# Sixteen-row substitution with a level of TensorE products, for four of six groups of a delta-rule kernel

## The chip, the cores and the metric

The kernel runs on one core of one Trainium2 chip. The metric is device time in microseconds (us) of one launch, median of the runs shown. The engines are called PE (TensorE, matmuls; PEld is its weight load), DVE (VectorE), ACT (ScalarE), POOL (GpSimd) and SP (SyncE, which issues most DMAs).

## What is computed

Two blocks, one after the other, in float32. The first is a delta-rule attention with 4 batches × 8 heads, 768 positions and 48 numbers a head:

```python
k_n = k / (norm(k) + 1e-06)
for t in range(S):
    y[:, :, t] = einsum('bhd,bhde->bhe', q[:, :, t], state)
    v_old = einsum('bhde,bhd->bhe', state, k_n[:, :, t])
    state = state + beta_t * einsum('bhd,bhe->bhde', k_n[:, :, t], v[:, :, t] - v_old)
```

The second takes the result as 3072 rows of 384, routes each row to the best of 8 experts by cosine similarity (argmax of softmax logits), and computes `gate * (relu(x @ w1[e]) @ w2[e])` with 1024 hidden numbers for that expert alone.

## The kernel before

**Chunks, groups, units.** The recurrence is solved by chunks of 64 positions (`C`), 12 of them (`m` = 0 to 11). Inside a chunk the values that enter the state solve a triangular system, whose matrix is made of products of keys. It is treated as two halves of 32 rows (`HC`): the inverses of the two diagonal 32×32 blocks are made explicitly, and the 32×32 corner between them is applied as a correction. Two chunks form a group (`g` = 0 to 5). A group holds 2 chunks × 32 heads × 2 halves = 128 blocks of 32×32, one for each of the 128 lanes of DVE. A unit `n` is one chunk of half of the batches; four units make a group, and unit `n` needs the state that unit `n` − 2 left.

**Preparing a group** (`prepare`). The keys are loaded, squared (ACT), summed (DVE), scaled (POOL; chunk 1 on DVE), transposed (PE) and moved out of PSUM by ACT. `gram_diag` makes the 32×32 blocks on PE, in 64 small matmuls a chunk. `to_lanes` (L553) transposes them on DVE, so that each lane has one block. POOL's `lower` (L558, L560) cuts the triangle and sets the diagonal to −1. Then comes the substitution: for each row j from 1 to 30 a `product` (L568) and a `subtract` (L572) on DVE, of (31 − j)·j elements in each lane. `from_lanes` (L580) transposes back, into WT, and two `spread` steps on ACT copy WT, with its two inner dimensions exchanged, into the left and the right half of W, each with a mask.

**A unit** is a chain of PE steps of 16 matmuls, with an engine between each two: `old` (keys by state), `rest` on DVE (R), `solve` with W, Y out on ACT, `fix` with the corner, U out on ACT, `solve_again` with W, Z out on ACT, `update`, and `new_state` on DVE. Beside the chain stand `gram`, `from_state`, `inside`, the transposes of the output rows, the logits, and the routing of every four units (`places`). All helpers of PE record their matmuls at L280 and those of ACT at L283, so steps are told apart by their tiles: R,W is `solve`, U,W `solve_again`, Y,Sx `fix`, Z,K `update`, S,KQ `old` or `from_state`; KQ with 48*32 is `gram_diag` and KQ with 48x96 `gram`.

**The order.** Each step is a task of `Plan.add(engine, busy, more, key, run, …)` with costs and a due key written by hand (`PERIOD`, the time planned for a unit, is 7.5). `Plan.order` walks through them with these costs and writes one fixed order for each engine, which is then executed first in, first out. A task with `hold` may make its engine stand a little for it. PSUM is four pairs of banks, which tasks take and give back. The substitution's tiles X and WT lie in the space of the first expert's `w2` until that is loaded; X has two buffers. X of a group is free for a later one when `from_lanes` has read it.

**After the last unit** the expert lists are completed, tokens are gathered and the expert stage begins (lines from L1190 on); two tiles of expert 0 are computed early, beside the last units (L1048, L1059).

Of the kernel before, what the change touches and what calls it, by code (L numbers as in the profile page):

```python
# [9 lines left out]
F32 = mybir.dt.float32  # L10
I32 = mybir.dt.int32
# [5 lines left out]

C = 64
HC = 32
T = 128  # L20
GROUP = 4
AHEAD_AT = 16
# [120 lines left out]
def kernel(  # L143
# [75 lines left out]
    def carved(n, shape, whole):  # L219
        size = shape[0] * shape[1] * (shape[2] if len(shape) > 2 else 1)  # L220
        return [whole[:, i * size:(i + 1) * size].rearrange(
            "p (a b c) -> p a b c" if len(shape) > 2 else "p (a b) -> p a b",
            **dict(zip("abc", shape))) for i in range(n)]
# [8 lines left out]
    buffers("rn", 2, [2, 2, NP, 2])  # L232
    buffers("rt", 2, [2, 2, NP, 2])
    quots = ac.tile([128, 2, 2, NP, 2], F32, name="quots")
    rings["X"], rings["WT"] = carved(2, [HC, HC], w2_flat), carved(3, [HC, HC], w2_flat)[2:]
    buffers("tmp", 2, [(HC // 2) * (HC // 2)])
    buffers("W", 2, [HC, C])
    buffers("Sx", 3, [H, C])
# [30 lines left out]
    def const(name, shape, dtype=F32):  # L269
        K[name] = ac.tile(shape, dtype, name=name)  # L270
        return K[name]
# [13 lines left out]


    ident = cpool.tile([128, 128], F32, name="ident")
    half_wide = cpool.tile([128, 256], F32, name="half")
    half = half_wide[:, 0:2 * GROUP * H]
    root = ac.tile([128, 1], F32, name="root")  # L290
    tiny = ac.tile([128, 1], F32, name="tiny")
    bt = rings["XC"][0].rearrange("p g r -> p (g r)")[0:40, 0:NM * 2 * C].rearrange("p (m o t) -> p m o t", m=NM, o=2)
# [57 lines left out]
    def masks():  # L350
        prow, col = K["prow"], K["col"]
        trow = const("trow", [128, C], I32)
        nc.vector.tensor_single_scalar(trow, prow, C - 1, op=ALU.bitwise_and)
        col_f = const("col_f", [128, C])
        nc.vector.tensor_copy(col_f, col)
        trow_f = const("trow_f", [128, C])
        nc.vector.tensor_copy(trow_f, trow)
        nc.vector.tensor_tensor(const("upper", [128, 1, C])[:, 0], col_f, trow_f, op=ALU.is_gt)
        nsec = const("nsecond", [128, 1])
        nc.vector.tensor_single_scalar(nsec, trow_f[:, 0:1], float(HC), op=ALU.is_ge)  # L360
        nc.vector.tensor_scalar_mul(nsec, nsec, -1.0)
        nc.vector.tensor_scalar(const("nfirst", [128, 1]), nsec, -1.0, -1.0, op0=ALU.mult, op1=ALU.add)
        for t in rings["Sx"]:
            nc.gpsimd.memset(t[:, :, 0:HC], 0.0)

    def load_beta():
        for i in range(2):
# [59 lines left out]
        return 4 * g * PERIOD  # L427

    def prepare(g):
        ms = (2 * g, 2 * g + 1)  # L430
        t0 = group_key(g)
        for m in ms:
            planned_k(m, t0 - 14 * PERIOD + (m % 2) * 2 * PERIOD if m > 1 else -200.0 + 0.5 * m)
        if g == 0:
            plan.add("SP", 1.6, 2.5, -199.8, load_beta, writes=["bt"])
            plan.add("DVE", 1.0, 0.2, -40.0, masks, reads=["iotas"], writes=["masks"])
            for ms_ in ((0, 1), tuple(range(2, NM))):
# [2 lines left out]
                         writes=[("beta_s", ms_[0])])  # L440
                plan.add("ACT", 0.4, 0.2, -140.0 if ms_[0] == 0 else -60.0, beta_root(slice(ms_[0], ms_[-1] + 1)),
                         reads=[("beta_s", ms_[0]), "half"], writes=[("sqb", a) for a in ms_])
        plan.add("DVE", 0.8, 0.2, t0 - 9.7 * PERIOD, beta_refine(slice(2 * g, 2 * g + 2)), reads=[("beta_s", min(2 * g, 2))],
                 writes=[("sqb", a) for a in ms] + ["quot"])
        ss, rt = buf("rn", g), buf("rt", g)

# [7 lines left out]
                nc.vector.tensor_reduce(ss[:, m % 2].rearrange("p i j jj -> p i (j jj)"), buf("sq", m), axis=AX.X, op=ALU.add)  # L454
            return step
        for m in ms:
            plan.add(*act(768), t0 - 12.5 * PERIOD + (m % 2) * PERIOD, square(m),
                     reads=[("k", m % 4, 0), ("k", m % 4, 1)], writes=[at("sq", m)])
            plan.add(*dve(768), t0 - 12 * PERIOD + (m % 2) * PERIOD, total(m),
                     reads=[at("sq", m)], writes=[at("rn", g) + (m % 2,)])  # L460

        def flat(t, part):
# [28 lines left out]
        for part in (slice(0, 1), slice(1, 2)) if g == 0 else (slice(0, 2),):  # L491
            xs = range(part.start, part.stop)
            those, roots_of = [at("rn", g) + (x,) for x in xs], [at("rt", g) + (x,) for x in xs]
            if g < 2:
                plan.add(*act(16 * len(xs)), t0 - 10 * PERIOD, roots_act(part), reads=those + ["half"], writes=roots_of)
            else:
                plan.add("POOL", 5.5, 0.2, t0 - 10 * PERIOD, roots(part), reads=those + ["half"], writes=roots_of)
            plan.add("DVE", 1.1 if g < 2 else 0.5, 0.2, t0 - 9.6 * PERIOD - (g == 0) * 30, scales(part), hold=g == 0,
                     reads=those, writes=roots_of + ["quots"])
            plan.add("DVE", 0.12 * len(xs), 0.2, t0 - 9.6 * PERIOD, scaled(part), hold=g == 0,  # L500
                     reads=[("sqb", 2 * g + x) for x in xs], writes=roots_of)

        def keys(m):
# [32 lines left out]
                                mm(p[r:r + HC, jj, to:to + w], KQ[rows, i, j, y, hf * HC:(hf + 1) * HC], KQ[rows, i, j, y, c:c + w])  # L536
            return step_
        for m in ms:
            plan.add(*(dve(850) if m == 1 else pool(768)), t0 - 9.2 * PERIOD + (m % 2) * PERIOD, keys(m), hold=g == 0,
                     reads=[("k", m % 4, 0), ("k", m % 4, 1), at("rt", g) + (m % 2,)], writes=[at("K", m)])  # L540
            plan.add(*pe(8, 0.11), t0 - 8.6 * PERIOD + (m % 2) * PERIOD, transposes("K", m, "KT"), mode=2,
                     reads=[at("K", m), "ident"], take=("KT", m))
            plan.add(*act(1024), t0 - 8.4 * PERIOD + (m % 2) * PERIOD, out_of_psum(m, "KT", slice(0, C)),
                     reads=[("psum", ("KT", m))], writes=[at("KQ", m) + ("K",)])
        for m in ms:
            first = m % 2 == 0
            plan.add(*pe(64, 0.02), t0 - 7.2 * PERIOD, gram_diag(m), mode=1, reads=[at("KQ", m) + ("K",)],
                     writes=[("X_next", g % 2)] + ([] if first else [("psum", ("diag", g))]),
                     take=("diag", g) if first else None)
        X = buf("X", g)  # L550

        def to_lanes():
            nc.vector.transpose(X, pair(("diag", g)).rearrange("p jj (x c) -> p c jj x", c=HC))  # L553
        plan.add(*dve(1024), t0 - 6.5 * PERIOD, to_lanes, hold=g == 0, reads=[("psum", ("diag", g))],
                 writes=[at("X", g), ("X_next", g % 2)])

        def lower():
            nc.gpsimd.affine_select(out=X, in_=X, compare_op=ALU.is_ge, fill=0.0, base=-1,  # L558
                                    pattern=[[1, HC], [-1, HC]], channel_multiplier=0)
            nc.gpsimd.memset(X.rearrange("p a b -> p (a b)")[:, ::HC + 1], -1.0)  # L560
        plan.add("POOL", 1.2, 0.1, t0 - 6.4 * PERIOD, lower, writes=[at("X", g)])

        for j in range(1, HC - 1):
            rows = HC - 1 - j
            t = buf("tmp", j)[:, 0:rows * j].rearrange("p (a b) -> p a b", b=j)

            def product(j=j, rows=rows, t=t):
                nc.vector.tensor_tensor(t, X[:, j + 1:, j:j + 1].broadcast_to([128, rows, j]),  # L568
                                        X[:, j:j + 1, 0:j].broadcast_to([128, rows, j]), op=ALU.mult)

            def subtract(j=j, rows=rows, t=t):
                nc.vector.tensor_tensor(X[:, j + 1:, 0:j], X[:, j + 1:, 0:j], t, op=ALU.subtract)  # L572
            key = t0 - (6.0 - j * 4.0 / HC) * PERIOD
            plan.add("DVE", rows * j / 960 + 0.085, 0.13, key, product, reads=[at("X", g)], writes=[at("tmp", j)], hold=g == 0)
            plan.add("DVE", rows * j / 960 + 0.085, 0.13, key + 0.01, subtract, reads=[at("tmp", j)], writes=[at("X", g)], hold=g == 0)

        WT, W = buf("WT", g), buf("W", g)

        def from_lanes():
            nc.vector.transpose(WT, X)  # L580
        plan.add(*dve(1024), t0 - 1.9 * PERIOD, from_lanes, reads=[at("X", g)], writes=[at("WT", g), ("X_next", g % 2)])
        for b, name in enumerate(("nfirst", "nsecond")):
            def spread(b=b, name=name):
                act_copy(W[:, :, b * HC:(b + 1) * HC], WT.rearrange("p i x -> p x i"), K[name])
            plan.add(*act(1024, True), t0 - 1.8 * PERIOD, spread, reads=[at("WT", g), "masks"], writes=[at("W", g) + (b,)])

    def x_of(m, jj, i, j):
        return ((jj * 2 + m % 2) * 2 + i) * NP + j
# [496 lines left out]
    for g in range(NG):  # L1085
# [5 lines left out]
        if g == NG - 1:  # L1091
            for i in range(NF, NF + 2 * KC):
                plan.add("SP", 0.4, 2.5, group_key(NG - 2) + 4.0 * i, first_weights(i),
                         writes=["w1_first"] + [("k", a, b) for a in range(4) for b in range(2)])
            for i in range(NF):
                plan.add("SP", 0.4, 2.5, group_key(NG - 1) + 2.0 * i, first_weights(i),
                         writes=["w2_first", ("X", 0), ("X", 1), ("WT", 0)])
        for n in range(4 * g, 4 * g + 4):
            unit(n)
            if n == groups[group_of[n]["n"]]["first"] + group_of[n]["G"] - 1:  # L1100
# [6 lines left out]
                early_tile(i, unit_key(AHEAD_AT + 6) + 2 * i * PERIOD)  # L1107
    def warm(p):
        for b in range(2):
            mm(p[HALF[b], b, 0:256], ident[:, HALF[b]], half_wide)  # L1110
    plan.emit(warm)
    lists = {-1: lists[groups[-1]["n"]]}
    att.close()
# [279 lines left out]
```

## Time and profile before

| | us |
|---|---|
| runs | 618.40, 620.38, 622.43 |
| median | 620.38 |
| profiled execution, its time | 617.46 |
| profiled execution, its span | 615.6 |
| first `solve` of unit 0 | 66.71 |
| first matmul of the expert stage (L1190) | 344.48 |
| mean granted PE clock, share of full speed | 0.900 |

The profile is one execution. Times in it count from its span's start. A group's row has the engine, the operation, out<-in by the program's names, partitions x elements, the count, the busy time in us and the mean duration in ns, then the idle time of the engine just before and what ended it; "issue" is idle time for which the profile shows no cause. One PE record is one pass: a step of 16 float32 matmuls has 32. "w_first" in a name is the space of the first expert's weights, where k, X and WT lie. The rows around the first use of the substitution, in order of time on DVE:

```profile
27.80 1.25 DVE L553 STREAM_TRANSPOSE w_first<-psum_pair 128x1024 f32<-128x1024 f32 x1 [1.79 <-PE psum_pair L280]
...
32.73 0.13 DVE L568 TENSOR_TENSOR tmp<-w_first 128x30 f32<-128x30 f32 x1
...
58.24 1.24 DVE L553 STREAM_TRANSPOSE w_first<-psum_pair 128x1024 f32<-128x1024 f32 x1
...
60.66 0.19 DVE L572 TENSOR_TENSOR w_first<-w_first,tmp 128x30 f32<-128x30 f32 x1
...
61.37 1.23 DVE L580 STREAM_TRANSPOSE w_first<-w_first 128x1024 f32<-128x1024 f32 x1
```

The first line fills the lanes of group 0, the third those of group 1, and the last takes group 0 back. On ACT the two spreads of group 0 follow at 62.64 (2.07 us) and 64.61 (2.04 us).

### The profile page before, as it was taken

The page shows a single profiled execution, that of the slowest core. Times are in us where ns is not written, and L with a number is a line of the kernel's source. Part 1 is how long each engine was busy: PE and PEld are TensorE (multiplying, and loading weights), DVE is VectorE, ACT ScalarE, POOL GpSimd, SP SyncE. Part 2 cuts the span into 40 slices and gives each one's busy share as a digit, 9 for nine tenths or more (in the row PEclk, how much of TensorE's full clock was granted, in tenths as well). Part 3 has the DMA queues.
Part 4 walks back from the last instruction along what each step waited for, and adds up shares of the span by engine and source line. Part 5 has one row for each costly group of instructions (what it writes and reads, how often), then busy time and mean ns, then how long its engine had stood idle before and what let it go on. Part 6 is the DMA issues. An engine that isn't in the chain of part 4 may idle for free. (4 is left out here: it accounts for less than half of the span.)

```text
span 615.6 us, 21947 instructions
## 1 busy us (share of the span) xinstructions
PE 516.1 (84%) x9643; PEld 425.9 (69%) x9643; DVE 275.9 (45%) x778; ACT 185.4 (30%) x343; POOL 168.5 (27%) x228
## 2 busy tenths in 40 slices
PE   3573688688797878888899599999999999999990
PEld 3462577578686767777887577887767777777870
DVE  4798777777789877962325121111011221121000
ACT  2331534634635536555442020111001221110110
POOL 4433426064534132230212212331202211111100
PEclk9965678667879897998899799999999999999996
DMA  4444734543341340032201599997637666679300
GB/s 81 75 82 82 198 72 71 105 99 70 65 100 32 90 135 18 19 101 66 85 31 43 184 383 384 382 370 256 227 139 245 187 207 237 209 254 338 131 15 18
DMA packets 116334, 90.55 MB, mean 147 GB/s; under 512 B 83394, under 2 KB 105308, under 8 KB 116226
## 3 DMA queue, kind: packets, MB, share of 16 engines
q1 hardware_dynamic: 110722, 77.76, 42.7%
q0 software_dynamic: 4416, 11.06, 5.1%
q8 instruction: 80, 1.31, 0.9%
q10 hardware_dynamic: 1088, 0.20, 0.2%
q14 instruction: 28, 0.23, 0.1%
HBM read 77.06 MB, written 12.13 MB: 145 GB/s over the span
## 5 line engine op out<-in xcount | busy, mean ns | idle before, releaser
L1200 PEld LDWEIGHTS acc<-xTm,w 128*128 128x128 f32 x576 | 77.7, 191 | 5.8 <-issue 1.8
L1202 ACT ACTIVATE hT<-acc 128x512 f32<-128x512 f32 (+3 forms) x52 | 28.5, 548 | 175.2 <-PE acc L1200 175.2
L1200 PE MATMUL acc<-xTm,w 128*128 128x128 f32 (+3 forms) x576 | 80.3, 299 | 0.0
L1217 PE MATMUL acc<-w,hT 128*128 128x384 f32 (+2 forms) x272 | 78.9, 489 | 0.0
L572 DVE TENSOR_TENSOR w_first<-w_first,tmp 128x30 f32<-128x30 f32 (+9 forms) x180 | 69.0, 385 | 3.9
L568 DVE TENSOR_TENSOR tmp<-w_first 128x30 f32<-128x30 f32 (+9 forms) x180 | 66.7, 372 | 4.1
L280 PE MATMUL psum_pair<-KQ 48*32 48x64 f32 (+2 forms) x2304 | 50.0, 265 | 18.9 <-issue 9.2
L1230 POOL DMA_INDIRECT out_dram<-y,more_ids x22 | 21.7, 986 | 160.5 <-DVE y L1220 127.4
L1217 PEld LDWEIGHTS acc<-w,hT 128*128 128x128 f32 (+2 forms) x272 | 42.2, 176 | 30.3 <-issue 5.8
L1191 DVE COPY xTm<-acc 128x384 f32<-128x384 f32 (+3 forms) x26 | 12.6, 508 | 109.1 <-PE acc L1190 104.5
L280 PEld LDWEIGHTS psum_pair<-KQ 48*32 48x32 f32 (+1 forms) x2304 | 42.4, 135 | 24.4 <-issue 12.1
L1220 DVE TENSOR_SCALAR y<-acc,xg 128x384 f32<-128x384 f32 x20 | 12.4, 618 | 97.7 <-PE acc L1217 93.2
L1200 PEld LDWEIGHTS acc<-xTm,w_first 128*128 128x128 f32 x288 | 44.6, 200 | 3.7 <-DVE y L1227 0.6
L1200 PE MATMUL acc<-xTm,w_first 128*128 128x128 f32 (+3 forms) x288 | 46.8, 325 | 0.4 <-DVE xTm L1191 0.4
L1217 PE MATMUL acc<-w_first,hT 128*128 128x384 f32 (+2 forms) x176 | 44.2, 489 | 0.0
L280 PE MATMUL psum_pair<-S,KQ 48*64 48x64 f32 x1408 | 35.6, 244 | 9.9 <-issue 4.7
L280 PEld LDWEIGHTS psum_pair<-S,KQ 48*64 48x64 f32 x1408 | 30.5, 155 | 13.4 <-issue 6.3
L283 ACT ACTIVATE KQ<-psum_pair 128x1024 f32<-128x1024 f32 x24 | 24.4, 1022 | 43.5 <-PE psum_pair L316 33.7
L973 POOL DMA_INDIRECT idmap<-tokid,slots_i x24 | 24.1, 1005 | 42.3 <-DVE slots_i L949 22.8
L1217 PEld LDWEIGHTS acc<-w_first,hT 128*128 128x128 f32 (+2 forms) x176 | 23.1, 163 | 17.8 <-issue 4.5
L622 POOL TENSOR_TENSOR V<-v,sqb 128x384 f32<-128x384 f32 x24 | 20.9, 876 | 48.8 <-DVE R L677 22.0
L469 POOL TENSOR_TENSOR rt<-rn,half 128x32 f32<-128x32 f32 x4 | 22.0, 5488 | 30.2 <-DVE rn L454 30.2
(207 smaller groups left out, 766.2 us busy)
## 6 DMA issues: line engine op xcount, KB each, us to landing
w<-in_moe_w_dram SPq DMA_DIRECT2D x24, 1536.0 KB
w_first<-in_moe_w_dram SPq DMA_DIRECT2D x10, 1536.0 KB
q<-in_q_dram SPq DMA_DIRECT2D x96, 48.0 KB
v<-in_v_dram SPq DMA_DIRECT2D x48, 96.0 KB
w_first<-in_k_dram SPq DMA_DIRECT2D x88, 48.0 KB
x_dram<-XC SPq DMA_DIRECT2D x5, 800.0 KB
idmap<-space SPq DMA_DIRECT2D x1, 2048.0 KB
w_first<-in_moe_w_dram SPq DMA_DIRECT2D x6, 256.0 KB
```

The source lines that it names most:

```text
L280: nc.tensor.matmul(out_, lhsT=lhsT, rhs=rhs, start=start, stop=True, skip_group_check=True)
L283: nc.scalar.activation(out_, in_, ACT.Copy, scale=scale)
L469: nc.gpsimd.tensor_tensor(out=flat(rt, part), in0=flat(ss, part), in1=half[:, 0:w], op=ALU.pow)
L568: nc.vector.tensor_tensor(t, X[:, j + 1:, j:j + 1].broadcast_to([128, rows, j]), X[:, j:j + 1, 0:j].broadcast_to([128, rows, j]), op=ALU.mult)
L572: nc.vector.tensor_tensor(X[:, j + 1:, 0:j], X[:, j + 1:, 0:j], t, op=ALU.subtract)
L622: nc.gpsimd.tensor_tensor(buf("V", m)[:, i * 2 * NP * D:(i + 1) * 2 * NP * D].rearrange("p (jj j d) -> p jj j d", jj=2, d=D), buf("v", m)[ ...
L973: put = nc.gpsimd.indirect_dma_start(out=idmap[:, :], out_offset=bass.IndirectOffsetOnAxis(ap=slot_i[:, i:i + 1], axis=0), in_=K["tokid"][ ...
L1191: nc.vector.tensor_copy(t.xT[:, :, b * T:b * T + n], psX[:, :, 0:n])
L1200: nc.tensor.matmul(psH[:, i, :], lhsT=t.w1[:, j, (f + i) * 128:(f + i + 1) * 128], rhs=t.xT[:, j, 0:t.width], start=(j == 0), stop=(j == K ...
L1202: nc.scalar.activation(t.hT[:, f:f + k, 0:t.width], psH, ACT.Relu)
L1217: nc.tensor.matmul(psO[c:c + w, :], lhsT=t.hT[:, f, b * T + o:b * T + o + w], rhs=t.w2[:, f, :], start=(f < q), stop=(f >= NF - q))
L1230: nc.gpsimd.indirect_dma_start(out=out[:, :], out_offset=bass.IndirectOffsetOnAxis(ap=t.ids[b][0:n, 1:2], axis=0), in_=y[0:n, :], in_offse ...
```

## The change

For groups 0, 1, 3 and 5 (`FINE`) the substitution runs in the two 16×16 diagonal blocks (`LC`) of each 32×32 block at once: j goes from 1 to 14, and each of the 28 operations covers both blocks, 2·(15 − j)·j elements. The 16×16 corner is then made by PE in two passes of 64 matmuls (`level_one`, `level_two`, each in two halves of 32), with 64 rows, 64 columns of weights and 16 moving columns. Their weights are W itself, filled for a while by ACT with the transposed first rows (`rows_spread`, two copies of 512); the result of the first pass comes out through ACT (`level_one_out`) into WN, and that of the second is added to WT by DVE (`merged`). After that the old spreads fill W. Groups 2 and 4 keep the 30 rows of substitution.

```diff
+LC = 16
+FINE = (0, 1, 3, 5)
-    rings["X"], rings["WT"] = carved(2, [HC, HC], w2_flat), carved(3, [HC, HC], w2_flat)[2:]
+    lanes = HC * HC + HC
+    rings["X"] = [w2_flat[:, 0:lanes]]
+    rings["WT"] = carved(1, [HC, HC], w2_flat[:, lanes:])
+    rings["WN"] = carved(1, [LC, HC], w2_flat[:, lanes + HC * HC:])
...
+        for t in rings["W"]:
+            nc.gpsimd.memset(t, 0.0)
...
+        if fine:
+            for j in range(1, LC - 1):
+                rows = LC - 1 - j
+                t = buf("tmp", j)[:, 0:2 * rows * j].rearrange("p (e a b) -> p e a b", e=2, b=j)
+                def product(j=j, rows=rows, t=t):
+                    nc.vector.tensor_tensor(t, blocks[:, :, j + 1:LC, j:j + 1].broadcast_to([128, 2, rows, j]),
+                                            blocks[:, :, j:j + 1, 0:j].broadcast_to([128, 2, rows, j]), op=ALU.mult)
+                def subtract(j=j, rows=rows, t=t):
+                    to = blocks[:, :, j + 1:LC, 0:j]
+                    nc.vector.tensor_tensor(to, to, t, op=ALU.subtract)
...
+        def rows_from_lanes():
+            nc.vector.transpose(WN, X.rearrange("p a b -> p b a")[:, 0:LC])
         def from_lanes():
+            if fine:
+                nc.vector.memset(X[:, LC:, 0:LC], 0.0)
             nc.vector.transpose(WT, X)
...
+                def rows_spread(b=b, name=name):
+                    act_copy(W[:, :, b * HC:b * HC + LC], WN.rearrange("p r x -> p x r"), K[name])
+            def level_one(xs):
+                    for x in xs:
+                        for o in range(2):
+                            mm(p[HALF[o], 0, x * LC:(x + 1) * LC], W[HALF[o], x], WT[HALF[o], LC:, x])
+            def level_one_out():
+                act_copy(WN.rearrange("p r x -> p (r x)"), pair(level)[:, 0], K["lo"])
+            def level_two(xs):
+                            mm(p[HALF[o], 1, x * LC:(x + 1) * LC], W[HALF[o], x], part[HALF[o], x * LC:(x + 1) * LC])
+            def merged():
+                nc.vector.scalar_tensor_tensor(out=to, in0=pair(level)[:, 1].rearrange("p (x c) -> p x c", c=LC),
+                                               scalar=K["lo"], in1=to, op0=ALU.mult, op1=ALU.add)
+            for a in range(2):
+                plan.add(*pe(32, 0.0335), L1 + 0.03 + a * 0.01, level_one(half_x[a]), reads=both + [at("WT", g)],
+                         writes=[("psum", level)] if a else (), take=None if a else level)
```

To make room for WN, X has one buffer in place of two. The due keys of a fine group's preparation move later by two PERIODs, since its substitution is shorter (`t0 = group_key(g) - (0 if fine else 2) * PERIOD`, with the numbers in the keys lowered by two, so those of groups 2 and 4 stay). A few masks are added, and a constant is made narrower. The planner then writes a new order for every engine: among others SP issues the keys of chunk 3 and 4 after q and v of chunk 0, and POOL clears both W buffers (`memset`) at the beginning.

## Prediction

> **What bounds the kernel now.** I read the page's busy line and slices first, to see where TensorE (PE) is not full.
>
> ```profile
> PE 516.1 (84%) x9643; PEld 425.9 (69%) x9643; DVE 275.9 (45%) x778; ACT 185.4 (30%) x343; POOL 168.5 (27%) x228
> PE   3573688688797878888899599999999999999990
> DVE  4798777777789877962325121111011221121000
> PEclk9965678667879897998899799999999999999996
> ```
>
> A slice is 15.4 us. From about 335 us on PE is at 9: that is the expert stage, which the change doesn't touch and which starts when routing ends. Before that DVE stands at 7 to 9 and PE at 5 to 8, part of it on a low clock. Next come the stages between the first solves of the six groups (a PE step that reads a new W starts each), and the tail.
>
> ```profile
> 0.00:66.70 66.70, 32.13 (x843) 27.19 (x843) 52.02 (x143) 20.33 (x27) 30.62 (x80) 0.76 0.45 80
> 66.70:116.50 49.80, 39.35 (x1292) 34.33 (x1292) 39.20 (x109) 24.25 (x43) 16.79 (x15) 0.81 0.51 113
> 116.50:165.10 48.60, 38.09 (x1280) 34.68 (x1284) 34.75 (x92) 23.74 (x39) 23.39 (x19) 0.75 0.44 91
> 165.10:212.00 46.90, 39.78 (x1422) 35.86 (x1416) 40.29 (x114) 23.30 (x43) 15.10 (x20) 0.90 0.31 73
> 212.00:253.50 41.50, 34.37 (x1307) 30.90 (x1310) 32.25 (x93) 18.78 (x34) 8.90 (x13) 0.84 0.25 62
> 253.50:289.80 36.30, 29.68 (x1140) 27.23 (x1130) 22.03 (x68) 20.37 (x40) 9.91 (x13) 0.95 0.23 72
> 289.80:335.00 45.20, 43.52 (x991) 37.95 (x991) 13.61 (x66) 18.60 (x51) 10.52 (x17) 0.96 0.16 50
> ```
>
> Columns: stretch, length, busy us of PE, weight load, DVE, ACT, POOL, then clock, DMA share, GB/s. Each stage but the last does the four units of one group and prepares a later one. The stage lasts 49.8 us while DVE is loaded and 36.3 when it isn't. Two lines are most of DVE's load:
>
> ```profile
> L572 DVE TENSOR_TENSOR w_first<-w_first,tmp 128x30 f32<-128x30 f32 (+9 forms) x180 | 69.0, 385 | 3.9
> L568 DVE TENSOR_TENSOR tmp<-w_first 128x30 f32<-128x30 f32 (+9 forms) x180 | 66.7, 372 | 4.1
> ```
>
> That is the substitution: 135.7 us, 22.6 a group. The timeline (start, us, engine, line; ACT rows, then PE rows) shows whether it is late.
>
> ```profile
> 112.43 2.09 ACT L283 ACTIVATE W<-w_first,nfirst 128x1024 f32<-128x1024 f32 x1 [2.75 <-DVE w_first L580]
> 114.43 2.02 ACT L283 ACTIVATE W<-w_first,nsecond 128x1024 f32<-128x1024 f32 x1
> ```
>
> ```profile
> 112.72 1.83 PE L316 MATMUL psum_pair<-ident,K 128*128 128x128 f32 x8 [0.71 <-DVE lz L792]
> 116.51 1.13 PE L280 MATMUL psum_pair<-R,W 64*64 64x64 f32 x32 [1.96 <-ACT W L283]
> ```
>
> For group 1 it is: PE stands until W is spread. The W of groups 0 to 5 were spread by 66.7, 116.5, 163.4, 202.1, 244.2 and 279.6, and first used at 66.7, 116.5, 165.1, 212, 253.5 and 289.8: groups 0, 1 and 2 wait on it, 3 to 5 have 9 us or more in hand. So the substitution ends last only in the first half, and later PE's own work does. From 66.7 to 335 PE is idle 43.5 us: 19.1 under "issue", 5.1 for W, 7.4 for Z (ACT, part of it behind the spreads), 6.6 for DVE, the rest small.
>
> **DVE.** For a fine group the 60 operations go. In their place come 28 with 28 to 112 elements; the rows of those sizes give 0.19 (30 elements) to 0.27 us (108) and the timeline 0.03 between them: 7.6 us. Added are a transpose of 512 (half of L580's 1.24: 0.65), a memset of 256 (0.27 at L336) and the merge of 512 out of PSUM (0.68, L659). Net 13.4 us off DVE, 54 over four groups. It counts only where DVE is late.
>
> **The start.** The transpose to lanes still ends at 29.1 and POOL's triangle at 30.7. Then 7.6 us of operations, with two totals (0.95 each), group 1's scales (2.3) and scaling (0.25) queued between them: 42.7. One total belongs to chunk 4, whose k now stands in SP's queue behind q and v of chunk 0 (8 loads take 5.2 us): issued until about 36, squared about 39, so some 2 us of standing, with the rest of the substitution queued behind: 44.7. Transposes and memset to 46.9, ACT's two 512-row spreads (half of 2.08 each) to 47.7. Now PE's order: the four new steps stand among two transposes of K (1.97 each), one of q (1.97) and two gram_diag (2.0 each). 9.9 us of queue, 4.8 of steps (below), 0.9 for the eviction, 0.9 for the merge, 4.1 for the old spreads: 68.5. On a full clock the transposes take 1.04, which saves 2.8: 65.7. I take 66, against 66.65: 0.7 gained of the 14 us that DVE saves; the queue ate it. Bounds 63 and 70. POOL's memset of both W (4096 elements; 512 took 0.52) is 4.2 us inside the 8.9 in which POOL waits before L506, and costs 4 where that gap is gone. The other moved loads have SP's lead as cover.
>
> **Stages 1 to 3.** Group 1's lanes should be filled at about 61 and its triangle be out at 63; 7.6 us of operations follow, with two copies of S between them that wait for units 0 and 1 (74.5 and 77.3 now), so they end near 80; transposes, spreads, four steps between unit steps and the merge make W1 some 15 us later, at 96, 20 us earlier than now. So the stages from 66.7 and 116.5 should fall to that from 212, the one whose W was in time beside a full substitution: 49.8 and 48.6 against 41.5, 15.4 us. That includes the cold run behind the stall (clock 0.50 from about 114 to 132). The stage from 165 has 5.4 over 41.5 with DVE 86% busy; its substitution turns fine; I take half, 2.7. Removed in all: 0.7 + 15.4 + 2.7 = 18.8.
>
> **PE's new work.** 128 matmuls a fine group, two records each (16 matmuls show as x32): 256, each with a load of 64 columns. No row has this shape. Low bound: gram_diag, 16 ns a record; high: the beta transposes, 64 columns with 8 moving, 39 ns.
>
> ```profile
> 176.66 2.14 PE L280 MATMUL psum_pair<-KQ 48*32 48x64 f32 x128
> 183.04 2.02 PE L280 MATMUL psum_pair<-KQ 48*32 48x64 f32 x128
> 10.54 5.55 PE L280 MATMUL psum_pair<-ident,XC 8*64 8x8 f32 x142 [1.15 <-DMA w_first<-in_k_dram]
> ```
>
> That is 4.0 to 10.0 us a group; I take 19 ns, 4.8 us, 1.2 a step, near gram_diag since it too is a run of small tiles on idle quarters. [...] Group 0's steps are in the start. The other three are 14.4 us in stages where PE idles 17% (7.1 of 41.5); the steps wait on one another, so the planner puts unit steps between, and I let half show: 7.2. The bounds are 0 and 30.
>
> **ACT and issue.** 1.04 + 1.04 + 0.65 = 2.7 us more ACT a fine group; unit evictions (Y, U, Z) queue behind, as Z does now (2.9 at 163). Now 7.4 us of Z waits go with 25 us of spreads; 8.1 more us at under that rate: 1.5. "Issue" idle, 19.1 us for some 14,900 PE instructions, grows with 1,536 more: 2.0. One X buffer in place of two serializes groups' substitutions; a fine one between two full ones leaves room (9 us in hand).
>
> **Sum.** 617.46 (span 615.6) − 18.8 + 7.2 + 1.5 + 2.0 = 609.4. The median of the runs, 620.38, is 2.9 above the profiled one: 612.
>
> **The clock.** It can undo this.
>
> ```profile
> 177.00:180.00 3.00, 2.97 (x118) 2.65 (x101) 1.60 (x5) 0.25 (x1) 2.40 (x4) 0.66 0.65 228
> 180.00:183.00 3.00, 3.00 (x97) 2.82 (x97) 2.61 (x6) 1.02 (x1) 1.50 (x3) 0.50 0.24 44
> ```
>
> PE is full here and its clock still falls, after gram_diag's small tiles; 64-wide steps then take 1.1 us, not 0.65. The new steps are small tiles too: one cold run of 8 us, some 4 lost, per group would add 12. [...]
>
> **Rivals.**
> - *DVE bounds all of it*: the stage from 165 gives all 5.4, the start its 3.7, and the new steps vanish in PE's idle time: −24.5 + 3.5, 596.5, as a median 599. For it: stage lengths follow DVE's load. Against: after 165 no W is late and PE idles just 6.6 us for DVE in all stages. 0.20.
> - *Slower, PE throughput*: the steps use two of the four quarters at a time and run at 27 ns, 6.9 a group, all of it shown: 20.7 + 3.5, and only the labelled waits go (5.1 for W, 6.6 for DVE, 3.7 of Z): +9, 627, as a median 629; with the clock's 12 more, 641. It decides from about 20 ns a record fully shown (3 × 5.1 + 3.5 = 18.8). For it: dense PE rows after 165, and the clock. 0.23.
> - *Given back*: W1 is early, but unit 2 and 3 wait behind level steps and spreads, and the 15.4 shrinks to 8: 617, as a median 620. 0.17. That the operations are not replaced is excluded by the order of instructions.
>
> **Numbers.** The forecast has 0.40, its own range 606 to 619. One per cent, 6.2 us, is about what a measurement tells from no change: faster is under 614.2, slower over 626.6. Of the forecast 0.27 falls under and 0.13 within; with the rivals faster 0.47, same 0.30, slower 0.23. 598 to 629 leaves out the slow rival's clock part and the fast one's better half.
>
> **What would show it.** Right: first solve at 63 to 70; W of group 1 spread by 90 to 100; unit 4's solve 8 us or more earlier than 116.5; level steps 1 to 1.5 us each; DVE busy near 222. Wrong: a step over 1.8 us, clock 0.5 behind the steps, or the stages from groups 3 and 5 on longer by more than 5 us.

## The result, and the profile after

The changed kernel took 663.96 us (median of 661.37 to 665.71) against 621.12 (618.40 to 622.43): a ratio of 1.071, 95% interval 1.066 to 1.075. It is slower by 43 us; the prediction said 612. The profiled execution shown here took 664.17, with a span of 662.4.

The busy line and the slices of the changed kernel:

```profile
PE 573.6 (87%) x10667; PEld 486.5 (73%) x10667; DVE 231.4 (35%) x667; ACT 196.0 (30%) x355; POOL 171.4 (26%) x230
PE   3639789888788988788899969999999999999990
DVE  4880563783373693281222241111001212121100
PEclk9999985888695698897868979999999999999996
```

DVE lost 44.5 us of work, for 54 predicted. PE gained 57.5 us and 1,024 records, and the stretch in which PE is not full (slices below 9, before the expert stage) has become longer, not shorter. The expert stage is as long as it was (272.2 us for 271.1); it only starts later, at 390.23 where it started at 344.48: 45.75 us. The stretches between the first solves of the groups say where (columns as in the prediction's table: stretch, length, busy us of PE, weight load, DVE, ACT, POOL, then clock, DMA share, GB/s; the last row ends at the first matmul of the expert stage):

```profile
0.00:78.68 78.68, 47.49 (x1100) 43.54 (x1100) 42.08 (x127) 23.01 (x30) 34.95 (x84) 1.00 0.50 103
78.68:132.80 54.12, 48.66 (x1461) 45.60 (x1464) 32.99 (x81) 24.42 (x40) 11.07 (x8) 0.75 0.30 54
132.80:182.45 49.65, 40.90 (x1380) 37.16 (x1376) 26.36 (x77) 25.17 (x43) 21.91 (x23) 0.79 0.44 89
182.45:239.53 57.08, 50.58 (x1621) 46.95 (x1616) 36.00 (x103) 24.02 (x42) 18.77 (x20) 0.76 0.21 46
239.53:283.73 44.20, 36.04 (x1375) 33.58 (x1369) 18.87 (x57) 21.47 (x39) 10.87 (x15) 0.88 0.29 77
283.73:329.14 45.41, 40.09 (x1295) 37.30 (x1287) 19.00 (x60) 21.75 (x40) 8.99 (x12) 0.85 0.21 63
329.14:390.23 61.09, 54.50 (x1104) 46.29 (x1104) 19.07 (x95) 20.14 (x55) 14.83 (x20) 0.88 0.14 42
```

The rows where a fine group's corner is made are the first, second, fourth and sixth: 78.7, 54.1, 57.1 and 45.4 us for 66.7, 49.8, 46.9 and 36.3. The third, without a corner, is as long as it was (49.7 for 48.6), although DVE has 8.4 us less to do there. The lengths no longer follow DVE's load; they follow PE's.

Two groups of the page show the exchange, the substitution's two-block subtract on DVE, and the corner's matmuls on PE:

```profile
L591 DVE TENSOR_TENSOR w_first<-w_first,tmp 128x28 f32<-128x28 f32 (+6 forms) x56 | 15.3, 273 | 1.4
...
L285 PE MATMUL psum_pair<-w_first,W 64*64 64x16 f32 x1024 | 55.0, 256 | 7.4 <-issue 6.7
```

The first was costed well: with its product (16.6) it is 8.0 us a group, 7.6 predicted. The second is the result. Four groups of 256 records take 55.0 us of PE, 54 ns a record; the prediction had 19. The time up to the expert stage, before and after (columns as above), shows how little hides it:

```profile
0.00:344.48 344.48, 261.79 (x8254) 230.69 (x8254) 238.86 (x708) 149.38 (x275) 118.47 (x177) 0.85 0.35 78
```

```profile
0.00:390.23 390.23, 318.27 (x9278) 290.42 (x9278) 194.37 (x597) 159.98 (x287) 121.40 (x179) 0.85 0.31 69
```

PE is busy 318.3 us where it was busy 261.8 (+56.5), and its idle time only falls from 82.7 to 72.0 (−10.7). These two make the 45.75.

The timeline of PE shows one group's steps (start, us; the first two rows are group 0, the others group 5):

```profile
52.90 3.60 PE L285 MATMUL psum_pair<-w_first,W 64*64 64x16 f32 x64
60.20 3.60 PE L285 MATMUL psum_pair<-w_first,W 64*64 64x16 f32 x64
...
302.48 1.75 PE L285 MATMUL psum_pair<-w_first,W 64*64 64x16 f32 x54 [0.90 <-issue]
304.63 2.04 PE L285 MATMUL psum_pair<-w_first,W 64*64 64x16 f32 x64
308.81 3.43 PE L285 MATMUL psum_pair<-w_first,W 64*64 64x16 f32 x61
```

A half step of 64 records takes 2.0 us at 304.63 and 3.4 us four us later. Windows of 3 us around it show what changed (clock is the number after POOL):

```profile
302.00:305.00 3.00, 2.52 (x69) 2.32 (x70) 0.00 (x0) 0.62 (x2) 0.00 (x0) 1.00 0.21 39
305.00:308.00 3.00, 3.00 (x68) 2.95 (x69) 0.00 (x0) 0.92 (x2) 0.99 (x1) 0.79 0.37 111
308.00:311.00 3.00, 3.00 (x74) 3.00 (x76) 0.17 (x1) 0.49 (x1) 0.97 (x1) 0.50 0.51 136
311.00:314.00 3.00, 3.00 (x76) 3.00 (x76) 0.00 (x0) 0.00 (x0) 0.00 (x0) 0.50 0.03 7
314.00:317.00 3.00, 3.00 (x74) 3.00 (x75) 0.25 (x1) 0.00 (x0) 0.00 (x0) 0.50 0.00 0
```

From 305 on PE is written as busy without a gap, and the granted clock falls from 1.00 to 0.50 and stays there. The records of the half step at 304.63 start 29 ns apart, those of the one at 308.81 53 ns. So a record costs 29 ns on the full clock and 53 on half, and most of the steps run on half: group 3's from 202 to 222, group 1's from 96 to 115, and by its times group 0's too (the clock written for that part is taken up at the end).

### The profile page after: what moved, and what is told of

It reads as the page before. It is cut to its first block, busy times and chain, and to the rows that moved or that the text cites. A ratio compares the mean times of both kernels' runs of the same rounds, so it can differ in the third digit from the quotient of the medians.

```text
span 662.4 us, 23917 instructions
## 1 busy us (share of the span) xinstructions
PE 573.6 (87%) x10667; PEld 486.5 (73%) x10667; DVE 231.4 (35%) x667; ACT 196.0 (30%) x355; POOL 171.4 (26%) x230
## 5 line engine op out<-in xcount | busy, mean ns | idle before, releaser
L285 PE MATMUL psum_pair<-KQ 48*32 48x64 f32 (+2 forms) x2304 | 51.7, 272 | 14.5 <-issue 13.1
L285 PE MATMUL psum_pair<-w_first,W 64*64 64x16 f32 x1024 | 55.0, 256 | 7.4 <-issue 6.7
L285 PEld LDWEIGHTS psum_pair<-w_first,W 64*64 64x64 f32 x1024 | 53.9, 211 | 8.7 <-issue 7.3
L285 PEld LDWEIGHTS psum_pair<-KQ 48*32 48x32 f32 (+1 forms) x2304 | 44.1, 140 | 19.2 <-issue 16.1
L1302 DVE TENSOR_SCALAR y<-acc,xg 128x384 f32<-128x384 f32 x20 | 12.4, 618 | 97.7 <-PE acc L1299 93.2
L285 PE MATMUL psum_pair<-S,KQ 48*64 48x64 f32 x1408 | 38.1, 256 | 7.0 <-issue 4.6
L285 PEld LDWEIGHTS psum_pair<-S,KQ 48*64 48x64 f32 x1408 | 32.9, 165 | 10.6 <-issue 6.0
L520 POOL TENSOR_TENSOR K<-w_first,rt 128x384 f32<-128x384 f32 x22 | 18.2, 848 | 46.0 <-DVE rt L502 24.5
```

The lines of the kernel that those rows point to most:

```text
L285: nc.tensor.matmul(out_, lhsT=lhsT, rhs=rhs, start=start, stop=True, skip_group_check=True)
L520: (nc.vector if m == 1 else nc.gpsimd).tensor_tensor(heads(buf("K", m))[:, i], buf("k", m)[:, i], rt[:, m % 2, i].rearrange("p j jj -> p ( ...
L1302: nc.vector.tensor_scalar_mul(y, psO, t.x[b][:, Dm:Dm + 1])
```

## The experiments

**Theories.** A: the loss is the steps' own PE time, and nothing hides it; a half step takes its records by the time of one tile, over the number of tiles that run at once, and twice that on half clock. B: the loss is the longer way to W, with more tasks in a fixed order over DVE, ACT and PE and one X buffer; PE's time would have fitted into its idle time.

Two of the kernels below compute another corner, and one none. The routing then sees other rows, and the expert stage has another length. For these three only times up to the first matmul of the expert stage are compared ("the start of the experts": 344.48 before, 390.23 after), not the whole.

**The same steps, with few records.** Each half step is two matmuls of 256 moving columns with the weights of one block:

```diff
-                    for x in xs:
-                        for o in range(2):
-                            mm(p[HALF[o], 0, x * LC:(x + 1) * LC], W[HALF[o], x], WT[HALF[o], LC:, x])
+                    h = slice(0, 256) if xs[0] == 0 else slice(256, 512)
+                    q = slice(0, 16) if xs[0] == 0 else slice(16, 32)
+                    for o in range(2):
+                        mm(p[HALF[o], 0, h], W[HALF[o], xs[0]], WT.rearrange("p c x -> p x c")[HALF[o], q, LC:])
```

> The changed kernel with each half step of level_one and level_two made of 2 matmuls of 256 moving columns in place of 32 of 16, the weights being those of one block alone (so the corner of the inverses is not the right one, and routing sees other rows). Every task, its waits, the two spreads of rows and the one X buffer stay; PE work of the steps falls from 1,024 records (55 us in the profile after) to 64. Theory A (the steps' own PE time, with the low clock around them, is the loss): the first matmul of the expert stage comes at 342 to 352 us in place of 390, the total at 615 to 628. Theory B (the loss is the longer way to W: more tasks over DVE, ACT and PE in a fixed order, and one X buffer; the matmuls mostly fill idle PE time): 650 to 664.

The whole took 764.3 us, outside what either theory said, because the other corner sent more tiles to the experts: their matmuls have 960 records on w where the kernel before has 576. I had not thought of that. Up to the experts the run answers the question. Its group and its first expert matmul:

```profile
L285 PE MATMUL psum_pair<-w_first,W 64*64 64x256 f32 x64 | 13.9, 516 | 0.8 <-ACT W L288 0.8
```

```profile
350.89 0.87 PE L1273 MATMUL acc<-ident,xg 128*128 128x128 f32 x3 [4.66 <-DMA xg<-x_dram,ids]
```

With 41.1 us less of PE in the steps, and every task, wait and buffer of the changed kernel still there, the experts start 39.3 us earlier. What is left over the kernel before is 6.4 us. (A second profile of the changed kernel, on another chip, has its steps at 56.9 us and its experts at 387.21: such differences hold to some 3 us.)

**Four quarters instead of two.** The same 1,024 records and columns, but the outputs of odd blocks go to the other half of the partitions, so that all four quarters of the array are used (the corner lands in the wrong place):

```diff
-                            mm(p[HALF[o], 0, x * LC:(x + 1) * LC], W[HALF[o], x], WT[HALF[o], LC:, x])
+                            mm(p[HALF[o ^ (x % 2)], o, x * LC:(x + 1) * LC], W[HALF[o], x], WT[HALF[o], LC:, x])
```

> The changed kernel with the level matmuls writing to the other half of the partitions for every odd block (and to the bank of their row half), so that four quarters of the array follow each other in place of two; count and sizes are the same, the sums go to places that are not read for them (the corner is not the right one). Theory A with the reason that two quarters alone share the work: a record takes 15 ns on the full clock and 28 on the low one, half of now, a half step 1.0 to 1.8 us in place of 1.9 to 3.6, and the total falls by 22 to 30 to 634 to 642. If the weights' load or the issue is the limit whatever the quarter, the steps stay at 1.9 to 3.6 us and the total at 660 to 667. Theory B: 655 to 664 although the steps get shorter.

The steps' group, and one half step on each clock:

```profile
L285 PE MATMUL psum_pair<-w_first,W 64*64 64x16 f32 x1024 | 28.8, 247 | 7.6 <-issue 6.6 <-ACT W L288 0.8
```

```profile
51.91 1.91 PE L285 MATMUL psum_pair<-w_first,W 64*64 64x16 f32 x64
...
282.32 1.12 PE L285 MATMUL psum_pair<-w_first,W 64*64 64x16 f32 x64
```

Half the time for the same records: 1.9 for 3.6 us, 1.1 for 2.0; the records start 26 and 14.5 ns apart, for 53 and 29. From these distances, times the number of quarters, my estimate is that a 64×64 tile with 16 columns holds its quarter for some 105 ns on half clock and 58 on full (4 × 26 and 2 × 53, 4 × 14.5 and 2 × 29). The edit also gives each row half a PSUM bank of its own, where both wrote into one, and no run takes the two apart; but the small tiles below write one bank from four row groups at 16 ns a record, so a shared bank alone does not hold a record for 53. The experts start at 362.14. The three kernels differ in their steps' matmuls alone: 13.9, 28.8, 55.0 us; starts 350.89, 362.14, 390.23. From the first to the second a us of step costs 0.75, from the second to the third 1.07 (0.89 with the second profile). That is A: little of it is hidden. (The whole, 679.3, again has other routing.)

**No fine group** (`FINE = ()`, all the rest of the change kept).

> The changed kernel with no fine group: all six groups with the full substitution, but with one X buffer, the memset of W and the masks of the change. Theory A: what is left of the change costs little, 616 to 630. Theory B in the part of the single X buffer (a group's lanes can be filled only when the group before has gone back, and W comes late): 635 to 660.

628.3 us, ratio 1.016 (1.010 to 1.022): about 10 us of the loss are not the corner's. Its PE has the records of the kernel before (9,643) but is busy 271.4 us up to the experts, not 261.8: it works at a lower clock (0.72 and 0.66 in the second and third stretch, 0.81 and 0.75 before), and is idle 0.8 us longer. Why the clock is lower isn't shown.

**The steps alone, in the kernel before.** 256 such matmuls for each of groups 0, 1, 3 and 5 as soon as their W is whole; only a small copy on DVE reads the result:

```diff
+            for i in range(4):
+                plan.add(*pe(32, 0.0335), t0 - 1.7 * PERIOD + 0.01 * i, level_step(half_x[i % 2], i // 2), reads=both + [at("WT", g)],
+                         writes=[("psum", level)] if i else (), take=None if i else level)
```

> The kernel before with the 256 level matmuls of each of groups 0, 1, 3 and 5 added after W is complete, as PE work that nothing in the computation waits for (one small DVE copy reads their PSUM so that it can be given back); the result is not changed. Theory A: the same 1,024 records cost about as much here, 30 to 50 us: 650 to 670. Theory B: they fill idle PE time and cost under 10: 621 to 631.

687.6 us, 69.5 more than the 618.07 of the kernel before on that chip: more than A said. The experts start 65.7 later: PE is busy 59.4 us longer up to there, of which the steps took 52.2, and idle 6.2 longer. PE's waits for W went from 5.1 to 18.3, since the steps stand in front of units' steps and wait for both spreads; other waits fell by about half of that. A names the greater part; the rest is B's, a wait of the place that I had chosen, and other matmuls that take longer.

The same place with four quarters, and with wide matmuls, separates the two without another routing:

> The kernel before plus 256 matmuls of the level's shape for each of groups 0, 1, 3 and 5, as in the run that took 687.6, but with the outputs in all four quarters of TensorE instead of two. Theory A: a half step falls from 3.5 us to 1.9 at half clock (1.0 at full clock), 22 to 28 us go, 658 to 668 us. Theory B (what costs is where the steps stand in the order and what they wait for): 678 to 690.

> The same, but each half step is two matmuls of 256 moving columns in place of 32 pairs of 16: the same places in the order, the same waits, the same 1,024 columns a step, a twentieth of the records. Theory A: own time 10 to 15 us in all in place of 52, so 630 to 648 us, and the clock after the steps back at 1.00 as it is in the changed kernel with wide matmuls. Theory B: 670 to 690.

This chip ran the kernel before in 635.2 us (630.3 to 639.6); the numbers in the expectations were for the other one, so differences are taken. Quarters: 680.1, +44.9 (ratio 1.065, 1.057 to 1.073), 24.6 less than with two quarters; steps 29.5, W waits 16.2. Wide: 664.3, +29.1 (1.043, 1.036 to 1.050), steps 17.2, W waits 18.3. Steps and added waits for W make 40.6 and 30.4, a rough sum, as other waits change too. The waits for W are nearly the same in all three, and the rest follows the steps' time. The wide steps missed the 10 to 15 us and, in group 1, the clock that the expectation gave them; more on that below.

**Two X buffers**, again with no fine group:

```diff
-    rings["X"] = [w2_flat[:, 0:lanes]]
+    rings["X"] = [w2_flat[:, 0:lanes], w2_flat[:, lanes:2 * lanes]]
...
```

> The changed kernel with no fine group (as in the run that took 628.3) and two X buffers again, WN's place given up. If the 10 us that the run without fine groups lies over the kernel before come from the one X buffer: 615 to 622 us. If they come from the moved loads, the cleared W buffers and the new order: 625 to 631.

637.8 against 635.2: 1.003 (0.999 to 1.007), for 1.016 with one buffer. So most of the 10 us, some 8 (3 to 12 by the two intervals), are the one buffer's; the moved loads, the clearing of W and the new order cost some 2 (−1 to 5). The two ratios are from two chips.

**Small tiles.** W is zero outside its 32×32 blocks, so each matmul can be cut into its two tiles of 32 rows and 32 columns, in four places of the array:

```diff
-                        for o in range(2):
-                            mm(p[HALF[o], 0, x * LC:(x + 1) * LC], W[HALF[o], x], WT[HALF[o], LC:, x])
+                        for b in range(2):
+                            for o in range(2):
+                                r = slice(o * C + b * HC, o * C + (b + 1) * HC)
+                                mm(p[r, 0, x * LC:(x + 1) * LC], W[r, x, b * HC:(b + 1) * HC], WT[r, LC:, x])
```

> The changed kernel with each 64x64 matmul of the level cut into its two 32x32 tiles on the diagonal (W is zero outside them): 512 records a fine group, four tiles at a time. Theory A (a us of the steps' own PE time is a us at the end, and a step's time is its records by the time of one tile over the number of tiles that run at once, as gram_diag's 16 ns a record): 512 x 16 ns = 8.2 us a group for the 14 measured, about 22 us off in all: 636 to 648 us, half steps of 1.9 to 2.2 us whatever the clock. Rival (a record costs what it costs, 28 to 55 ns each): 14 to 28 us a group, 664 to 715 us. Theory B (order and waits): no change, 658 to 668.

The ratio was 1.061 (1.053 to 1.069), a miss: the steps did take what A said, 33.9 us, but the time hardly fell. It was run again beside the changed kernel itself:

> The changed kernel, unchanged, beside the next one on one chip: ratio to the kernel before 1.066 to 1.075.

> The level in 32x32 tiles again, now on the chip of the changed kernel. Its steps had 33.9 us of PE busy time for 55.0, but 51 us of 'issue' idle for 27, at distances of 128 records. If instructions arrive no faster than these steps use them up, the gain is about 0 to 8 us: ratio to the kernel before 1.055 to 1.07, and the 'issue' idle time before the expert stage again 45 to 55 us against 25 to 32 in the changed kernel. If the stalls were that chip's alone: the gain is 18 to 24 us, ratio 1.03 to 1.045.

660.3 for the changed kernel and 657.2 with tiles (1.067, 1.060 to 1.073, and 1.062, 1.054 to 1.070). PE's longest waits up to the experts, columns us in total, times, longest; the changed kernel first, then tiles:

```profile
PE psum_pair L285 <- issue: 27.7, 25, 3.4
```

```profile
PE psum_pair L285 <- issue: 45.3, 42, 5.2
```

PE is busy 297.2 us for 316.1, which saves 18.9, and waits 17.6 more under "issue". The timeline of the tiles shows where:

```profile
56.28 1.04 PE L285 MATMUL psum_pair<-w_first,W 32*32 32x16 f32 x85
59.29 0.82 PE L285 MATMUL psum_pair<-w_first,W 32*32 32x16 f32 x43 [1.97 <-issue]
...
64.04 1.35 PE L285 MATMUL psum_pair<-w_first,W 32*32 32x16 f32 x85
70.59 0.82 PE L285 MATMUL psum_pair<-w_first,W 32*32 32x16 f32 x43 [5.19 <-issue]
```

PE stops in the middle of a step, and the profile shows no cause. Counted over the records, these stops come at distances of 128, or of a multiple of it, within a few. The instruction queue moved 88 packets of 16.4 KB in the changed kernel and 96 with tiles, 8 more for 1,024 more records: one for each 128. A step of 128 such records takes 1.91 us where nothing stops it (at 50.76), 15 ns a record. The trace also holds these packets: each of the 37 stops of over 0.3 us before the experts, 0.41 to 5.19 us long, ends 1.2 to 1.6 us after one of them has landed, and so do all 22 in the changed kernel and all 22 in the kernel before. Stops 128 records apart (such as those that end at 197.20, 200.66 and 204.11) come no closer than 3.45 us in the three traces: 27 ns a record, whatever the tiles could do. That PE waits there for its next instructions is my reading of these distances and packets; no view names the cause.

**The relief alone.** The changed kernel without the corner (no rows_from_lanes, rows_spread, steps or merge) and with two X buffers, beside the kernel before on the same chip:

> The kernel before, unchanged, for its trace on the chip of this call: the expert stage starts at 340 to 348 us where the chip is like that of the first profile, at 358 to 366 where it is like that of the last call (there the run with two X buffers started it at 363).

> The changed kernel without the corner: no rows_from_lanes, rows_spread, level steps or merge (the 16x16 corners stay zero, so the routing sees other rows and only times up to the expert stage are compared), and two X buffers. It has DVE's relief and nothing of its price. The prediction's step 'stages 1 to 3 shrink by 15.4 and 2.7': the expert stage starts 20 to 28 us earlier than in the kernel before on this chip. If PE's own work and clock set the stages' length and W was not late for much: 0 to 8 us earlier.

The kernel before started its experts at 344.48 and took 617.4. The relief alone, its first solve and its first expert matmul:

```profile
55.94 0.69 PE L285 MATMUL psum_pair<-V,W 64*64 64x64 f32 x32
```

```profile
325.37 0.87 PE L1231 MATMUL acc<-ident,xg 128*128 128x128 f32 x3 [4.56 <-DMA xg<-x_dram,ids]
```

19.1 us earlier, 11.3 of them at the start (55.94 for 67.22) and 7.8 after it; the expectation had asked for 20. (The whole, 641.3, has other routing.) The relief of DVE is real, and that its total meets the 18.8 of the sum is luck: the sum had 0.7 for the start, with the steps in it, and 18.1 for stages 1 to 3. These gave 8.7, 0.5 and 3.2, 12.4 in all, and the stage after them became 5.4 longer.

The changed kernel on the same chip starts its experts 61.8 us later than the relief alone. PE's time up to there, the relief first:

```profile
0.00:325.37 325.37, 252.56 (x8254) 227.24 (x8254) 186.92 (x589) 149.26 (x275) 121.08 (x179) 0.90 0.36 82
```

```profile
0.00:387.21 387.21, 316.08 (x9277) 287.92 (x9278) 194.07 (x597) 159.93 (x287) 121.85 (x179) 0.79 0.30 69
```

PE is busy 63.5 us longer, 56.9 of them in the steps and 6.6 in other matmuls, on a lower clock (0.82 for 0.89 in the mean from 80 us on); its idle time is 71.1 us for 72.8. So the steps filled under 2 us of PE's idle time.

None of this leads to a version that is faster than the kernel before: with steps cheaper than any that make the corner here (13.9 us) the experts still start 6.4 us later than in the kernel before, and giving back the second X buffer is worth some 8 of 618. That one was not tried, since WN takes the place of that buffer.

## Why the prediction was wrong

**The failed step is "PE's new work": 19 ns a record, 4.8 us a group, of which half shows.** Both halves of it failed.

- *The price.* 55.0 us in four groups is 13.8 a group. I took the price next to gram_diag's 16 ns, "since it too is a run of small tiles on idle quarters". gram_diag's weights are 32 columns wide and its tiles stand in all four quarters, eight places of 32 columns; the new ones are 64 wide and stand in two quarters. The run with four quarters halved the time at equal records (28.8 us for 55.0), so what counted here is the time that a tile holds its place, by the estimate above some 105 ns on half clock, over the places at work. The upper bound, 39 ns from the beta transposes, was also too low. The half clock does not explain that one: a transpose of K right behind them takes 1.97 us (at 17.67), as on half clock (1.95 us for the same shape at 129.28, on 0.50; 1.04 at 156.84, on 1.00). Which of the differences (8 rows and 8 moving columns for 64 and 16, among others) does, no run shows.
- *The cover.* "PE idles 17%", and the steps should have slipped half into it. But PE's idle time is waits at given places of a fixed order, and a step fills it only if it stands there with its inputs ready. PE's idle time fell by 10.7 us in all while DVE had 44 us less work until the experts; without the steps it fell by 11.4 (84.2 to 72.8 on one chip). So it was the relief that shortened it, the steps filled next to none of it, and a us of step cost 0.75 to 1.07.

**The clock**, left to a rival at 12 us, belongs in the price: the steps run on 0.50 while PE is busy without a gap, as group 3's do from 205 to 217 below. With wide matmuls at the same place the clock comes back within the steps here. Changed kernel with wide matmuls, group 3's steps, at 182.4 to 187.8:

```profile
182.00:185.00 3.00, 3.00 (x69) 1.93 (x71) 1.25 (x1) 0.49 (x1) 1.12 (x1) 0.50 0.49 91
185.00:188.00 3.00, 3.00 (x135) 2.66 (x136) 2.69 (x5) 1.65 (x3) 2.65 (x6) 0.95 0.03 8
```

The changed kernel, group 3's steps:

```profile
205.00:208.00 3.00, 3.00 (x78) 3.00 (x76) 2.10 (x8) 0.49 (x1) 0.07 (x1) 0.50 0.02 2
208.00:211.00 3.00, 3.00 (x78) 3.00 (x80) 0.00 (x0) 0.63 (x1) 0.00 (x0) 0.50 0.02 5
211.00:214.00 3.00, 3.00 (x72) 3.00 (x68) 0.00 (x0) 1.03 (x3) 0.00 (x0) 0.50 0.03 5
214.00:217.00 3.00, 3.00 (x78) 3.00 (x78) 0.13 (x1) 0.00 (x0) 0.16 (x1) 0.50 0.00 0
```

Both runs come to the steps on 0.50, and unit steps stand between theirs. With the wide ones the clock is back after some 4 us of busy PE; with the small ones it isn't after eighteen. Width alone does not decide it either. The kernel before with wide steps, where those of group 1 stand, from 128.9 to 138.2:

```profile
129.00:132.00 3.00, 3.00 (x17) 2.17 (x13) 1.39 (x5) 1.11 (x3) 0.00 (x0) 0.50 0.33 55
135.00:138.00 3.00, 3.00 (x18) 1.89 (x16) 0.17 (x1) 1.11 (x2) 2.54 (x6) 0.50 0.59 106
```

So busy PE does not tell the clock: all eight rows have PE busy for 3.00 of 3.00 us, seven at 0.50 and one at 0.95. What the clock goes by, no run here shows.

**The start**: 66 predicted, 78.68 measured, above its bound of 70. The part before the steps was right (DVE's transposes began at 44.0 and PE's first step at 47.5, for 44.7 and 47.7 predicted; the prediction's terms add up to 68.3, not 68.5, which changes nothing). Then come 14.2 us of steps for the 4.8 in the sum, and one stop of 3.3 us under "issue" inside the last step: 12.7 more, the miss. With wide steps the first solve is at 63.8, within the bounds, and without a corner at 55.9.

**Stages 1 to 3**: W of group 1 was to be spread by 90 to 100; it was spread from 116.49 to 120.57, so no relief reached unit 4, which starts at 132.80, 12 us later still, behind unit steps that leave PE no gap above 1.6 us. For this the steps are to blame, not the reading of DVE: with wide steps W is spread by 98.2. Yet the 15.4 us then don't come: unit 4 still starts at 112.06, 48.3 us after the first solve; W is now early, and units 2 and 3 wait on ACT (3.4 us right behind its spreads, 2.7 later). That was the rival "given back". Without any corner the two stretches are 43.3 and 47.0 for 52.1 and 47.5 in the kernel before on the same chip, 9.2 of the 15.4. The second hardly shrinks, and the prediction's reading of it was wrong: group 2 doesn't wait for W. W was spread at 163.4, the solve came at 165.09, and PE's wait before it is for Z, whose copy stands behind the spreads on ACT:

```profile
163.78 0.70 PE L280 MATMUL psum_pair<-Z,K 64*48 64x64 f32 x32 [2.86 <-ACT Z L283]
165.09 1.10 PE L280 MATMUL psum_pair<-R,W 64*64 64x64 f32 x32
```

Of the 7.1 us that the sum took from this stretch, the relief alone brings 0.5.

**One X buffer** was costed at nothing, with 9 us in hand as cover. It costs some 8.

**ACT and issue** were 1.5 and 2.0 in the sum. Neither showed so: PE's waits for ACT fell from 22.4 to 10.7 us, and its waits under "issue" are 23.0, 31.4 and 27.7 us in the kernel before, the relief alone and the changed kernel on one chip, so they don't grow with the number of records.

**DVE** was said to fall to near 222 and stands at 231.4: the transpose of 512 took 1.07 us (0.65 estimated) and the merge 1.13 (0.68). No run shows a cost of it.

**The rivals.** "Slower, PE throughput" named the cause, two of four quarters at a time and all of it shown, with 27 ns a record, which no row of the kernel before shows: about right on the full clock (29) and half of the 53 that most steps paid. Its 641 with the clock was 23 short, and its 23% too little: the prediction's own bounds held a price of twice the one chosen, and its clock rows stood beside it. The signs named for a wrong forecast came: steps of 3.6 us, clock 0.50 behind them, and the stages in which the corners of groups 3 and 5 are made longer by 10.2 and 9.1 (those that begin with the first solves of 3 and 5 became 2.7 and 6.4 longer).

**The account** for the 45.75 us at the start of the experts: relief −19.1; to the wide steps +25.5, of which their PE time is 13.9 and the X buffer some 8, the rest (ACT's and DVE's tasks for the corner, the order) not taken apart; from wide to the real steps +39.3. The terms come from runs on three chips.

## What to carry to other kernels

Price small matmuls by the time one tile holds its place in the array, over the places that work at once (here, by estimate, some 105 ns on half clock over two quarters), and price it on the clock that they will run on (29 ns a record on full clock here, 53 on half); a row with another weight width or other places is no near neighbour (16 ns for gram_diag, 54 for the steps). Work moved to an engine that is the next bound was paid nearly in full here: its idle time in a stage counts as cover only where a named wait, with the moved work's inputs ready, stands in the order. Before trading an engine's work for another's, run the relief without its price: it bounds what the trade can bring, here 19 us against a price of 65.

## What the hardware showed

- The granted clock stayed at 0.50 for 18 us in which PE was busy without a gap, some 13 of them with 64×64 tiles of 16 columns. With 256-column matmuls at the same place it was back within some 4 us; in another kernel it stood at 0.50 in two stretches of 3 us with PE busy for all of them, with such matmuls among others (129 and 135 us).
- 32×32 tiles ran at 10 ns a record on full clock (1.05 us for 104) and 16 on half (1.57 for 100), and PE stopped between them under "issue", up to 5.19 us at a time, at distances of 128 records or a multiple, and each stop of over 0.3 us ended 1.2 to 1.6 us after a packet of the instruction queue.
- In the first 70 us the profile writes clock 1.00 in the changed kernel, yet a half step takes 3.60 us and a transpose of eight matmuls 1.97 us there, as on half clock. A second profile of the same kernel, with the same 3.60 us, writes 0.50 there, so the clock's record in that part of the first isn't to be relied on:

```profile
50.00:53.00 3.00, 3.00 (x32) 2.63 (x31) 0.00 (x0) 0.60 (x1) 0.00 (x0) 0.50 0.36 66
53.00:56.00 3.00, 3.00 (x57) 2.96 (x56) 0.00 (x0) 0.43 (x1) 0.00 (x0) 0.50 0.39 71
```

- One chip ran the kernel before in 635.2 us, two others in 618; with nearly the same code (no fine group) the expert stage took 270.8 and 271.8 us on the slower and a faster chip, so the difference lay in the attention.
